# The last zero fill of a copy-bound kernel, dealt to fifteen of the sixteen DMA engines

**The chip, the cores and the metric.** One core of a Trainium2 chip. The metric is device microseconds (us) of one execution. Every timed execution here agreed within 0.3% with the others of its kernel and counts as undisturbed ("fast"), except the single runs of the last experiment, which are marked there. The times of one series come from one chip; the two timed series of experiments ran on two different chips.

## The reference

A single token goes through layernorm, attention over the last 4096 positions of a key and value cache, a residual, and a gated feed-forward network. The kernel must return the output row and eight gradients. Cut to what matters here:

```python
def _A_ref(x, k_cache, v_cache, wq, wo):
    Hq, Dh = 16, 256
    Hkv, Sk = k_cache.shape[1], k_cache.shape[2]      # 8, 32768
    W = min(4096, max(256, Sk // 4))                   # 4096
    k = jnp.repeat(k_cache[:, :, Sk - W:, :], rep, axis=1)
    v = jnp.repeat(v_cache[:, :, Sk - W:, :], rep, axis=1)
    ...
def reference(...):
    _out, _vjp = jax.vjp(_f, A_x, A_k_cache, A_v_cache, A_wq, A_wo, B_w_gate, B_w_up, B_w_down)
    _grads = _vjp(grad_out)
    return (_out0, *[jnp.asarray(_g) for _g in _grads])
```

The gradients of both caches have the shape of the caches, 1x8x32768x256 in bf16, and all but the last 4096 positions of each head are zero. Most of what the kernel writes is therefore zeros.

## The kernel before

A zero fill is a store of 128 rows of 8192 elements (`ZW`; 2 MB, 16,384 bytes in a row) from a tile of zeros in on-chip memory. GpSimd (`ZQ`) sends 103 of them, SyncE (`LD`) sends nearly all loads (ScalarE a few), all stores of results and the last few fills. Cuts are marked by `...`.

```python
ZW = 8192
HALF0, HALF1 = 42, 55
...
zeros = ar(0, ZW)                       # 128 partitions x ZW
...
late_jobs = [(out_2, G - 1, 5, 7, 2 * ZW), (out_3, G - 1, 0, 6, 2 * ZW), (out_3, G - 1, 6, 7, ZW)]
fills = []                              # the other 103 fills, [128, ZW] each
...
def send_fills(n0, n1, halves=False):
    for reg in fills[n0:n1]:
        if halves:
            ZQ.dma_start(out=reg.rearrange("p (k f) -> p k f", k=2),
                         in_=zeros[:, 0:ZW // 2].unsqueeze(1).to_broadcast([128, 2, ZW // 2]))
        else:
            ZQ.dma_start(out=reg, in_=zeros)

send_fills(0, HALF0)                    # 42 at the start
send_fills(HALF0, HALF1, True)          # 13 from half the tile
...
            if n == 1:                  # after the second block of the feed-forward part
                nc.vector.memset(ar(ZW // 2, ZW // 2), 0.0)
                send_fills(HALF1, len(fills))               # 48 more
...
for it, g in enumerate(order):          # backward, one key/value head at a time
    ...
    for o_ap, st_ in ((out_3, stV), (out_2, stK)):
        LD.dma_start(out=o_ap[0, g, Sk - W:, :].rearrange("(p t) d -> p t d", t=T), in_=st_)
    for job in plan[it]:
        job()
...
for o, g, n0, n1, f in late_jobs:       # the last stores of all
    reg = zero_rows(o, g, n0, n1, f)
    for i in range(reg.shape[0]):
        LD.dma_start(out=reg[i], in_=ar(2 * ZW - f, f))
```

Of the kernel before, what the change touches and what calls it, by code (L numbers as in the profile page):

```python
# [26 lines left out]
ZW = 8192  # L27
HALF0, HALF1 = 42, 55
# [5 lines left out]
def kernel(  # L34
# [4 lines left out]
    ZQ = nc.gpsimd  # L39
# [14 lines left out]
    def ar(off, n):  # L54
        return arena[:, off:off + n]
# [4 lines left out]
    zeros = ar(0, ZW)  # L60
# [54 lines left out]
    def zero_rows(o, g, n0, n1, f):  # L115
        reg = o[0, g, 0:Sk - W, :].rearrange("s d -> (s d)")[n0 * 128 * ZW:n1 * 128 * ZW]
        return reg.rearrange("(n p f) -> n p f", p=128, f=f)

    late_jobs = [(out_2, G - 1, 5, 7, 2 * ZW), (out_3, G - 1, 0, 6, 2 * ZW), (out_3, G - 1, 6, 7, ZW)]
    fills = []  # L120
# [7 lines left out]
# [3 lines that stand above are left out]
                ZQ.dma_start(out=reg.rearrange("p (k f) -> p k f", k=2), in_=zeros[:, 0:ZW // 2].unsqueeze(1).to_broadcast([128, 2, ZW // 2]))  # L131
            else:
                ZQ.dma_start(out=reg, in_=zeros)  # L133
# [212 lines left out]
    def block_views(n):  # L346
        f0, nb = BLOCKS[n]
        w = 128 * nb
        wgu = ar(wgu_off[n % 2], 8 * w).rearrange("p (c i f) -> p c i f", c=4, i=2)
        wd = ar(wd_off[n % 2], nb * D).rearrange("p (b n) -> p b n", n=D)  # L350
        return f0, nb, w, wgu, wd

    def load_block(n):
        f0, nb, w, wgu, wd = block_views(n)
        for eng, i, wt in ((LD, 0, B_w_gate), (nc.scalar, 1, B_w_up)):
            eng.dma_start(out=wgu[:, 0:3, i, :], in_=wt[0:384, :].rearrange("(c p) f -> p c f", c=3)[:, :, f0:f0 + w])
            eng.dma_start(out=wgu[0:DQ, 3, i, :], in_=wt[384:D, f0:f0 + w])
        LD.dma_start(out=wd, in_=B_w_down[f0:f0 + w, :].rearrange("(p b) n -> p b n", b=nb))
# [4 lines left out]
    with tc.tile_pool(name="ps_mid", bufs=3, space=bass.MemoryType.PSUM) as ps_mid, \  # L363
# [34 lines left out]
        for n in range(len(BLOCKS)):  # L398
            f0, nb, w, wgu, wd = block_views(n)
            b0 = f0 // 128  # L400
            cs = slice(b0, b0 + nb)
            for b in range(nb):
                nc.vector.tensor_tensor_reduce(out=dgb[:, 0:D], in0=wd[:, b, :], in1=dh2_bc[:], scale=1.0, scalar=0.0,
                                               op0=ALU.mult, op1=ALU.add, accum_out=d_hh[:, b0 + b:b0 + b + 1])
            gu_ps = ps_mid.tile([128, 2, 5], f32, tag="mid", name="gu_ps")
            for i in range(2):
                for b in range(nb):
                    for k in range(4):
                        kp = DQ if k == 3 else 128
                        nc.tensor.matmul(gu_ps[:, i, b:b + 1], lhsT=wgu[0:kp, k, i, b::nb], rhs=X2_b[0:kp, k:k + 1], start=(k == 0), stop=(k == 3))  # L410
            nc.vector.tensor_copy(out=gu_f[:, :, cs], in_=gu_ps[:, :, 0:nb])
            for i in range(2):
                nc.vector.tensor_tensor(out=dgu_f[:, i, cs], in0=d_hh[:, cs], in1=gu_f[:, 1 - i, cs], op=ALU.mult)
            nc.vector.tensor_tensor(out=hh_f[:, cs], in0=gu_f[:, 0, cs], in1=gu_f[:, 1, cs], op=ALU.mult)
            nc.vector.tensor_copy(out=hh_bf[:, cs], in_=hh_f[:, cs])
            for i in range(2):
                nc.vector.tensor_tensor(out=diag[:, 0:w].rearrange("p (m b) -> p m b", b=nb), in0=ident_f[:].unsqueeze(2).to_broadcast([128, 128, nb]),
                                        in1=dgu_f[:, i, cs].unsqueeze(1).to_broadcast([128, 128, nb]), op=ALU.mult)
                for m in range(2):
                    bc_ps = ps_mid.tile([128, 320], f32, tag="mid", name="bc_ps")  # L420
                    nc.tensor.matmul(bc_ps[:, 0:w // 2], lhsT=ones_bf[:], rhs=diag[:, m * w // 2:(m + 1) * w // 2], start=True, stop=True)
                    nc.scalar.copy(out=dgb[:, w * i + m * w // 2:w * i + (m + 1) * w // 2], in_=bc_ps[:, 0:w // 2])
            for b in range(nb):
                nc.tensor.matmul(ffn_ps[:], lhsT=hh_bf[:, b0 + b:b0 + b + 1], rhs=wd[:, b, :], start=(b0 + b == 0), stop=(b0 + b == NF - 1))
            for c in range(4):
                kp = DQ if c == 3 else 128
                wc = wgu[0:kp, c].rearrange("p i f -> p (i f)")
                nc.vector.tensor_tensor_reduce(out=wc, in0=wc, in1=dgb[0:kp, 0:2 * w], scale=1.0, scalar=0.0,
                                               op0=ALU.mult, op1=ALU.add, accum_out=dhn[0:kp, c, n:n + 1])
            if n + 2 < len(BLOCKS):  # L430
                load_block(n + 2)
            if n == 1:
                nc.vector.memset(ar(ZW // 2, ZW // 2), 0.0)
                send_fills(HALF1, len(fills))

        dcat2 = workm.tile([128, 8], f32)
        nc.vector.reduce_sum(out=dcat2[:, 0:4], in_=dhn[:], axis=AX)
# [57 lines left out]
    with tc.tile_pool(name="work2", bufs=2) as work2, tc.tile_pool(name="lnw", bufs=1) as lnw, \  # L495
# [109 lines left out]
        for it, g in enumerate(order):  # L605
# [50 lines left out]
            if it == 6:  # L656

                nc.vector.memset(ar(ZW, ZW), 0.0)

        for o, g, n0, n1, f in late_jobs:  # L660
            reg = zero_rows(o, g, n0, n1, f)
            for i in range(reg.shape[0]):
                LD.dma_start(out=reg[i], in_=ar(2 * ZW - f, f))
# [29 lines left out]
```

## Time and profile before

| | before |
|---|---|
| time, median (lowest to highest) | 798.80 us (798.65 to 799.12), 3 runs |
| span of the profiled execution | 797.2 us |
| moved by DMA | 334.76 MB, of them 280.59 MB written to memory |
| TensorE / VectorE / ScalarE busy | 60% / 55% / 25% |
| DMA engines busy | full until the last of forty slices |

No computing engine is busy for much more than half of the span, and the sixteen DMA engines are busy all the time. When the work is spread over sixteen servers that are all busy, an average rate tells nothing more: what matters is how ragged the end is, that is, how far apart the sixteen finish. The prediction below shows the lines for this, and how the ragged end is read: an engine alone is a share of 0.06 in the last stretches, and the last store's semaphore shows sixteen landings at the end. In the trace of before each of them comes 0.32 to 0.38 us after the end of one of the sixteen streams described next (the first streams end at 785.88 and 786.23 us, the first landings are at 786.22 and 786.55; the last 795.65 and 796.03), so they are read as one from each engine.

One piece of the reading is used throughout. The packets in the trace carry no engine number. But for 88% of the packets of 8,192 bytes or more between 400 and 780 us in the trace of before (8,376 of 9,478), some packet ends 3 to 4 ns after their start, and at 340 of 380 instants looked at there sixteen packets are in flight (at the others 17 or 18). This is read as one engine's next packet beginning 3 to 4 ns before the one before it ends, so packets can be strung into sixteen *streams*. A stream has no number either, but odd-sized packets can give one away. Where several packets end within a few ns, the order of the copies in each queue has to decide which stream goes on where, so a stream is an inference.

### The profile page before, as it was taken

The numbers are of one execution on the slowest core, as the hardware profiler recorded it, in microseconds if no ns is written. First come the engines' busy times: TensorE is split into PE (matmuls) and PEld (weight loads), VectorE is DVE, ScalarE is ACT, GpSimd is POOL, SyncE is SP. The second block draws the span as 40 slices with busy tenths as digits, with TensorE's granted clock in tenths as the row PEclk, the third lists the DMA queues.
The fourth block names the chain that finished last, engine by engine and source line by source line (L and its number), as shares of the span: only waits on it lengthen the run. The fifth ranks groups of instructions, "written<-read, shape, count | busy, mean of one in ns | idle before, by whom it ended". The sixth has DMA issues, their size and how long they took to land.

```text
span 797.2 us, 7318 instructions
## 1 busy us (share of the span) xinstructions
PE 478.9 (60%) x2926; PEld 222.6 (28%) x2926; DVE 437.1 (55%) x629; ACT 196.0 (25%) x309; POOL 61.8 (8%) x112
## 2 busy tenths in 40 slices
PE   0459999999999999251409478684450553722000
PEld 0334434344344333121208334331220211310000
DVE  2116584765846782263690679579653784964000
ACT  0142314134132201010102126353330442534000
POOL 4000000010101111100210001010000000000000
PEclk9989999999999999555558779766555556765555
DMA  9999999999999999999999999999999999999995
GB/s 349 431 430 430 428 431 430 430 428 430 430 423 427 427 419 413 423 421 424 432 428 423 424 431 431 428 425 427 424 424 422 424 424 424 423 427 418 433 434 247
DMA packets 29352, 334.76 MB, mean 420 GB/s; under 512 B 2819, under 2 KB 5894, under 8 KB 7814
## 3 DMA queue, kind: packets, MB, share of 16 engines
q0 software_dynamic: 16496, 216.01, 64.0%
q1 hardware_dynamic: 11382, 116.68, 34.8%
q10 hardware_dynamic: 1440, 1.61, 0.6%
q8 instruction: 23, 0.38, 0.2%
q14 instruction: 11, 0.09, 0.0%
HBM read 53.69 MB, written 280.59 MB: 419 GB/s over the span
## 4 chain that ended last, share of the span: by engine, by line
PE 37%; DMA 32%; DVE 16%; ACT 4%; issue 2%; another core or an unknown queue 0%; SPq 0%; DVEq 0%; ACTq 0%
DMA out_dram<-arena 19%; PE M_ps L317 12%; PE ok_ps L320 7%; PE rows_ps L256 6%; PE tr_ps L253 4%; DMA dh_bc<-in_grad_out_dram 4%; DMA arena<-in_A_k_cache_dram 4%; DMA arena<-in_B_w_down_dram 3%; ACT arena L270 2%; DVE arena L635 2%; DVE arena L459 2%; PE dqb_ps L502 2%; DMA arena<-in_B_w_gate_dram 2%; DVE arena L650 2%; PE d_ps L643 2%
## 5 line engine op out<-in xcount | busy, mean ns | idle before, releaser
L312 DVE TENSOR_TENSOR arena<-arena,p_f 128x2048 bf16<-128x2048 bf16 x64 | 145.4, 2286 | 61.6 <-PE M_ps L317 61.5
L317 PE MATMUL M_ps<-arena 128*128 128x512 bf16 x512 | 128.9, 380 | 0.2 <-ACT arena L323 0.2
L643 PE MATMUL d_ps<-arena,rT 32*128 32x512 bf16 x256 | 46.6, 529 | 111.0 <-DVE arena L651 63.9
L253 PE MATMUL tr_ps<-ident_bf,arena 128*128 128x128 bf16 x1024 | 92.5, 242 | 19.6 <-ACT arena L611 11.2
L256 PE MATMUL rows_ps<-arena,vpad 128*16 128x512 bf16 x256 | 90.6, 451 | 19.9 <-DVE arena L613 14.6
L133 POOL DMA_DIRECT2D out_dram<-arena x90 | 48.6, 542 | 538.5 <-DMA out_dram<-arena 491.3
L253 PEld LDWEIGHTS <-arena 128*128 128x128 bf16 x1024 | 69.0, 108 | 73.8 <-issue 64.4
L270 ACT COPY arena<-tr_ps 128x1024 bf16<-128x1024 bf16 x64 | 61.8, 1015 | 64.7 <-PE tr_ps L253 64.7
L647 ACT CAST arena<-d_ps 128x512 bf16<-128x512 f32 x64 | 37.7, 589 | 128.4 <-PE d_ps L643 128.3
L320 PE MATMUL ok_ps<-arena 128*16 128x512 bf16 x256 | 63.8, 381 | 0.9 <-DVE arena L297 0.9
L317 PEld LDWEIGHTS <-arena 128*128 128x128 bf16 x512 | 43.3, 99 | 59.0 <-issue 23.2
L611 ACT COPY arena<-tr_ps 128x1024 bf16<-128x1024 bf16 x32 | 32.6, 1019 | 94.6 <-PE tr_ps L253 36.4
L650 DVE CAST arena<-d_ps 128x512 bf16<-128x512 f32 x64 | 43.8, 684 | 16.9 <-PE d_ps L643 16.4
L651 DVE CAST arena<-d_ps 128x512 bf16<-128x512 f32 x64 | 43.5, 679 | 11.2 <-DMA out_dram<-arena 11.2
L643 PEld LDWEIGHTS <-rT 32*128 32x128 bf16 x256 | 11.2, 96 | 136.5 <-issue 90.0
L648 ACT CAST arena<-d_ps 128x512 bf16<-128x512 f32 x64 | 38.1, 595 | 11.9 <-DMA out_dram<-arena 11.9
L635 DVE TENSOR_TENSOR arena<-R_sb,tl_f 128x4096 bf16<-128x4096 bf16 x8 | 35.4, 4419 | 0.7 <-ACT R_sb L633 0.7
L256 PEld LDWEIGHTS <-vpad 128*16 128x16 bf16 x256 | 19.1, 92 | 58.4 <-issue 51.3
L320 PEld LDWEIGHTS <-arena 128*16 128x16 bf16 x256 | 19.1, 89 | 41.6 <-issue 20.5
L514 DVE CUSTOM_DVE_ANT_0 arena<-arena 128x4096 bf16<-128x4096 bf16 x3 | 13.1, 4423 | 23.9 <-ACT arena L507 23.9
L285 ACT ACTIVATE e_f<-cols_ps,nbias 128x32 f32<-128x32 f32 x16 | 4.5, 286 | 86.8 <-DVE nbias L281 86.8
L258 DVE COPY arena<-rows_ps 16x512 f32<-16x512 f32 x16 | 10.8, 676 | 26.6 <-PE rows_ps L256 26.6
(198 smaller groups left out, 387.9 us busy)
## 6 DMA issues: line engine op xcount, KB each, us to landing
out_dram<-arena POOLq DMA_DIRECT2D x103, 2048.0 KB, 51.7
out_dram<-arena SPq DMA_DIRECT2D x18, 2048.0 KB, 32.3
arena<-in_A_v_cache_dram SPq DMA_DIRECT2D x10, 2048.0 KB, 50.0
arena<-in_A_k_cache_dram SPq DMA_DIRECT2D x8, 2048.0 KB, 29.2
out_dram<-arena SPq DMA_DIRECT2D x4, 4096.0 KB, 43.8
arena<-in_A_wq_dram SPq DMA_DIRECT2D x2, 3072.0 KB, 20.6
arena<-in_A_wo_dram SPq DMA_DIRECT2D x2, 1792.0 KB, 14.5
out_dram<-arena SPq DMA_DIRECT2D x2, 1792.0 KB, 15.1
```

The lines of the kernel that those rows point to most:

```text
L133: ZQ.dma_start(out=reg, in_=zeros)
L253: nc.tensor.transpose(tr_ps[:, dh, i, :], X_sb[:, 4 * q + i, dh * 128:(dh + 1) * 128], ident_bf[:])
L256: nc.tensor.matmul(rows_ps[:], lhsT=pad[:, dh, 16 * q:16 * q + 16], rhs=XT[:, dh].rearrange("p t k -> p (t k)"), start=(q == 0 and dh == 0 ...
L270: sT_ps = dots(kv_at(K_off[g]), KT_slot, vpad[g % 2], rows1, ps_c, "cols", lambda q, XT, ps: nc.scalar.copy(out=XT, in_=ps))
L312: nc.vector.tensor_tensor(out=pK, in0=K_sb[:, 4 * c:4 * c + 4, :].unsqueeze(2).to_broadcast([128, 4, 2, Dh]), in1=p_f[:, c::8, :].unsqueez ...
L317: nc.tensor.matmul(M_ps[:, vh, :], lhsT=V_sb[:, t, vh * 128:(vh + 1) * 128], rhs=pK[:, i, :, :].rearrange("p h d -> p (h d)"), start=(t == ...
L320: nc.tensor.matmul(ok_ps[:].rearrange("p k d -> p (k d)"), lhsT=ppad[g % 2][:, 8 * (t % 4) + t // 4, :], rhs=both(g, t), start=(g == 0 and ...
L635: nc.vector.tensor_tensor(out=RB_, in0=R_sb[:].unsqueeze(1).to_broadcast([128, 8, 512]), in1=tl_f[:].unsqueeze(2).to_broadcast([128, 8, 51 ...
L643: nc.tensor.matmul(d_ps[:, qi].rearrange("p w d -> p (w d)"), lhsT=rT[32 * q:32 * (q + 1), :], rhs=RB_[32 * q:32 * (q + 1), l, :], start=T ...
L648: nc.scalar.copy(out=stK[:, t:t + 2, :], in_=d_ps[:, :, 1, :])
L650: nc.vector.tensor_copy(out=stV[:, t:t + 2, :], in_=d_ps[:, :, 0, :])
L651: nc.vector.tensor_copy(out=stK[:, t:t + 2, :], in_=d_ps[:, :, 1, :])
```

## The change

The intent: one of the sixteen engines is slower than the others and ends last. So the last of GpSimd's 103 fills is taken out of the loop, and sent at the very end in four parts that put rows on all engines but that one.

```diff
@@ -431,7 +431,7 @@
                 nc.vector.memset(ar(ZW // 2, ZW // 2), 0.0)
-                send_fills(HALF1, len(fills))
+                send_fills(HALF1, len(fills) - 1)
@@ -657,6 +657,14 @@
                 nc.vector.memset(ar(ZW, ZW), 0.0)
+        flat = fills[-1].rearrange("p f -> (p f)")
+        base = 0
+        for p0, k, m, w in ((0, 5, 2, 288), (20, 3, 8, ZW), (64, 8, 9, ZW - 40), (0, 4, 8, ZW)):
+            n = k * m * w
+            ZQ.dma_start(out=flat[base:base + n].rearrange("(k m f) -> k m f", k=k, m=m),
+                         in_=zeros[p0:p0 + 4 * k - 3:4, 0:w].unsqueeze(1).to_broadcast([k, m, w]))
+            base += n
+        assert base == 128 * ZW
         for o, g, n0, n1, f in late_jobs:
```

A tuple (p0, k, m, w) is one copy: m rows of w elements from each of k partitions p0, p0 + 4, p0 + 8 and so on. The engines are numbered here, as names: 0-4 (two tiny rows each), 5-7 (8 rows), 8-15 (9 rows, 40 elements shorter) and again 0-3 (8 rows). Engine 4 is the one that gets two rows of 576 bytes and no more. The stream with the two 896-byte stores is called engine 0.

## The prediction

> **What bounds the kernel now.** I read the page first, then busy time by stretch at the end, then GpSimd's timeline, and last the single landings and packets in the trace. The slices and queues of the page:
>
> ```profile
> PE   0459999999999999251409478684450553722000
> DMA  9999999999999999999999999999999999999995
> DMA packets 29352, 334.76 MB, mean 420 GB/s; under 512 B 2819, under 2 KB 5894, under 8 KB 7814
> q0 software_dynamic: 16496, 216.01, 64.0%
> q1 hardware_dynamic: 11382, 116.68, 34.8%
> ```
>
> The DMA engines are full in 39 of 40 slices, while TensorE has nothing to do in the last three. So the kernel is a copy: 334.76 MB (of which 216 MB zero fills from GpSimd on q0) over sixteen engines. What an engine does in which order hardly matters; the end is when the engine with most work left is done. The last stretches, in 1 us steps (us, five engines' busy time, clock, DMA share, GB/s):
>
> ```profile
> 782.00:784.00 2.00, 0.00 (x0) 0.00 (x0) 0.00 (x0) 0.00 (x0) 0.00 (x0) 0.50 0.97 418
> ...
> 788.00:789.00 1.00, 0.00 (x0) 0.00 (x0) 0.00 (x0) 0.00 (x0) 0.00 (x0) 0.50 0.65 279
> 789.00:790.00 1.00, 0.00 (x0) 0.00 (x0) 0.00 (x0) 0.00 (x0) 0.00 (x0) 0.50 0.27 115
> 790.00:791.00 1.00, 0.00 (x0) 0.00 (x0) 0.00 (x0) 0.00 (x0) 0.00 (x0) 0.50 0.12 49
> ...
> 793.00:794.00 1.00, 0.00 (x0) 0.00 (x0) 0.00 (x0) 0.00 (x0) 0.00 (x0) 0.50 0.11 49
> 794.00:795.00 1.00, 0.00 (x0) 0.00 (x0) 0.00 (x0) 0.00 (x0) 0.00 (x0) 0.50 0.04 16
> 795.00:796.00 1.00, 0.00 (x0) 0.00 (x0) 0.00 (x0) 0.00 (x0) 0.00 (x0) 0.50 0.04 16
> ```
>
> One engine is a share of 1/16 = 0.06. From 790 to 794 us two engines run (0.12), after that one, and the span ends at 797.2. The sixteen landings of the last store (its semaphore's events, in us from the span's start) say the same engine by engine: 786.2, 786.6, 787.2, 787.8, 787.8, 788.0, 789.2, 789.2, 789.5, 789.6, 789.8, 789.9, 790.4, 791.4, 794.4, 796.0. Their mean is 789.6, so perfect balance would be worth 796.0 - 789.6 = 6.4 us and no more. I call the last engine Z, the one of 794.4 Y, the one of 791.4 X.
>
> A packet of 16,384 bytes takes 0.611 us in the full stretches and also when Z runs alone, so an engine's own rate binds, and a row taken from Z is worth the same 0.611 us whenever it would have run.
>
> **Who Z is.** The packets carry no engine number, but on one engine the next packet starts 3 to 4 ns before the one before it ends, so they can be strung into sixteen streams, with the known order of every queue as a check. I followed them back from the end to 370 us. Z is not the stream with the two 896-byte stores of single rows (386 and 475 us)[...]. Z has no instruction fetch there, but its packets take 620 to 670 ns instead of 611 from 380 us on, when other engines' mostly do not: 5.9 us in all against 0.8 to 3.0 us on the others. Z is a steadily slow engine, not an unlucky one. The fetches[...] go round a set of eight streams, among them Y and X but neither Z nor engine 0.[...] The trace does not show that Z is the fifth (number 4); that the change aims so precisely at it is my main reason to believe it.
>
> [...]
>
> **The change, part by part.** The last of the 48 fills after the second block (128 rows of 16,384 bytes, 8 per engine) goes; four copies come, with k = 5, 3, 8, 4[...]. [...]engines 0 to 4 get 2 rows of 576 bytes each; 5 to 7 get 8 rows of 16,384; 8 to 15 get 9 rows of 16,304; 0 to 3 get 8 rows of 16,384. All 2 MB are covered.[...]
> - Engine 4: minus 8 x 0.611 = 4.89 us, plus 2 tiny packets, estimated at 0.04 us each from the 896-byte ones (41 ns). Net minus 4.8 us.
> - Engines 0 to 3 and 5 to 7: unchanged to 0.1 us.
> - Engines 8 to 15: 9 x 16,304 - 8 x 16,384 = 15,664 bytes more, 15,664 / 16,384 x 0.611 = 0.58 us[...].
>
> So if Z is engine 4 it lands at 796.0 - 4.8 = 791.2. The end then passes to Y: 794.4 if Y is in 0 to 7 (gain 1.6 us), 794.4 + 0.6 = 795.0 if it is in 8 to 15 (gain 1.0 us). X, at most at 792.0, is no issue. Two thirds of what is taken from Z is thus wasted.
>
> **GpSimd and the waits.** The last fills in GpSimd's timeline before:
>
> ```profile
> 664.67 0.53 POOL L133 DMA_DIRECT2D out_dram<-arena  x1 [9.41 <-DMA out_dram<-arena]
> 676.83 0.54 POOL L133 DMA_DIRECT2D out_dram<-arena  x1 [11.62 <-issue]
> ```
>
> It issues its last fill at 677 and is then idle. Four issues at 0.54 us are 2.2 us instead of 0.54, beside everything else. The built program shows new waits in front of the four: on VectorE's row copy (L258) and ScalarE's last transposed copy (L611) of the last group, which stand at about 701 us in the trace of before. So the fill comes some 25 us later. That costs nothing: in before the two preceding fills land at 718.6 and 724.7 us (median of their engines), SyncE's queue alone has work to 786, and the four need about 5 us of every engine somewhere before that. No other engine's instructions change place. SyncE's stores of the last groups may land up to 5 us sooner, which moves work but takes none away.
>
> **The rivals.**
> - *Aimed well, Y in 0 to 7*: gain 1.6 us, 797.2. *Aimed well, Y in 8 to 15*: gain 1.0 us, 797.8.[...]
> - *The wrong engine.*[...] Then Z keeps its 8 rows or gets 9: 798.8 to 799.5[...].
> - *Piled up.* If [...]each began at engine 0, engines 0 to 2 would get 8 + 9 + 8 rows instead of 8: 17 x 0.611 = 10.4 us more. Engine 0, ending at about 789.2, would land at about 799.6, and the time would be some 802.5. If Z were one of them, 809.
> - *A wait becomes the bound.* The four wait for late work; were SyncE's queue empty by then, they would be exposed. At 732 us, when TensorE is done, that queue is full to about 755, and its last stores are issued by 744, so I give this almost nothing.
>
> **Range and chances.** The timed runs spread by 0.5 us and sit 1.6 us above the span. I give the two aimed cases together 0.65 (797.2 and 797.8), the wrong engine 0.25 (798.8 to 799.5), piling up 0.07, anything else 0.03. The median of this is 797.8, and 797.0 to 799.5 holds a little over 8 in 10. Two per cent is 16 us, and the whole tail holds 6.4, so faster by 2% is out of reach. Slower by 2% needs the rows to collapse onto one or two engines.
>
> **What would show it.** Right: the last store's landings have a last value near 794.4 to 795.0 with the second near 792, one engine's share of 0.06 in the final 3 us in place of two engines' 0.12 at 790 to 794; the landings of eight engines 0.6 us later; on q0 the last 128 large packets on fifteen streams and none of them on Z. Wrong: a last landing still at 796.0 or later with Z having its 8 or 9 rows (wrong engine), or landings of three engines near 800 (piled up).[...]

That Z is engine 4, and that the four copies lie on the engines named, was not shown when the prediction was made. The rival *the wrong engine* is that the four copies spare another engine than Z. The stream with the two 896-byte stores, which the prediction goes on to call engine 0, lands at 789.2 us. The instruction fetches meant are the 23 packets of 16,384 bytes on q8, of the page's kind "instruction"; whose program they bring the page does not say.

The forecast's sum: Z lands at 796.0 - 8 x 0.611 + 2 x 0.04 = 791.2 us, so the end passes to Y, at 794.4 us or, with 0.58 us more, 795.0; that is 1.6 or 1.0 us off the 798.8 of before, 797.2 or 797.8 us.

## The result

| | before | after |
|---|---|---|
| time, median (lowest to highest), 4 runs each | 798.96 us (798.65 to 799.29) | 797.41 us (796.93 to 798.00) |
| span of the profiled execution | 797.2 us | 795.1 us |
| last landing / the one before it | 796.0 / 794.4 us | 794.0 / 793.3 us |
| mean of the sixteen landings | 789.6 us | 790.4 us |

The ratio is 0.9981, with a 95% interval of 0.9964 to 0.9998: a small gain of about 1.5 us, far within 2%. A ratio here is the mean time of one kernel's fast runs over that of the other's of the same rounds, so it isn't quite the ratio of the medians quoted.

The page of the kernel after, its DMA slices and queues:

```profile
DMA  9999999999999999999999999999999999999997
DMA packets 29688, 334.77 MB, mean 421 GB/s; under 512 B 3150, under 2 KB 6230, under 8 KB 8150
q0 software_dynamic: 16832, 216.01, 64.2%
q1 hardware_dynamic: 11382, 116.68, 35.0%
```

The same bytes are moved. The last slice is fuller, 7 tenths in place of 5: the engines now end closer together. There are 336 packets more on q0, and most are tiny: 320 more of 4 bytes (median 9 ns) and 11 of 8 bytes. In the kernel before, q0 has 1,648 packets of 4 bytes, one for each of 103 copies on 16 engines. After, it has 1,968, which are 272 beyond one for each of 106 copies on 16 engines, and 272 is 13 x 8 + 8 x 9 + 12 x 8: one for each row that the other engines got. For the first copy the 11 packets of 8 bytes fit, as many as there are other engines. So by these counts an engine without a share is not wholly idle, though at 9 ns a packet it is nearly so.

The last stretches of the kernel after, in the columns of the prediction (us, busy time of the five engines, clock, DMA share, GB/s):

```profile
788.00:789.00 1.00, 0.00 (x0) 0.00 (x0) 0.00 (x0) 0.00 (x0) 0.00 (x0) 0.50 0.77 328
789.00:790.00 1.00, 0.00 (x0) 0.00 (x0) 0.00 (x0) 0.00 (x0) 0.00 (x0) 0.50 0.54 229
790.00:791.00 1.00, 0.00 (x0) 0.00 (x0) 0.00 (x0) 0.00 (x0) 0.00 (x0) 0.50 0.31 131
791.00:792.00 1.00, 0.00 (x0) 0.00 (x0) 0.00 (x0) 0.00 (x0) 0.00 (x0) 0.50 0.31 131
792.00:793.00 1.00, 0.00 (x0) 0.00 (x0) 0.00 (x0) 0.00 (x0) 0.00 (x0) 0.50 0.08 33
793.00:794.00 1.00, 0.00 (x0) 0.00 (x0) 0.00 (x0) 0.00 (x0) 0.00 (x0) 0.50 0.04 16
```

Before, two engines ran alone from 791.1 us on. Now the share at 790 to 792 us is 0.31, about five engines' worth (5/16), and it falls to nothing within two more microseconds. The view counts whole packets: 0.08 is two packets of 0.61 us in one microsecond (2 x 0.61 / 16). The long tail of one engine is gone, and several others have taken its place.

GpSimd's timeline of the kernel after (start, us, engine, line, operation, number, and what ended the idle time before):

```profile
667.53 0.53 POOL L133 DMA_DIRECT2D out_dram<-arena  x1 [9.18 <-DMA out_dram<-arena]
701.35 1.94 POOL L664 DMA_DIRECT2D out_dram<-arena  x3 [33.30 <-DVE arena L651]
708.78 0.60 POOL L664 DMA_DIRECT2D out_dram<-arena  x1 [5.48 <-DMA out_dram<-arena]
```

The last ordinary fill goes out at 667.5 us and the four parts at 701 to 709 us, as foreseen. The releaser named in the brackets is inferred; the prediction read the waits, on VectorE's L258 and ScalarE's L611, from the built program.

**Which stream is which.** The last fill leaves marks, for on each group of engines its rows have another size. Five streams carry a packet of 1,152 bytes (two rows of 576 sent as one; 51 ns): they are engines 0 to 4. Eight carry nine packets of 16,304 bytes: 8 to 15. The one stream that has the 1,152-byte packet and no large row of this fill is engine 4. It is also the slow one: between 468 and 492 us, 36 of its 38 packets of 16,384 bytes took over 618 ns (Z before: 34 of 38), on the other fifteen streams together 5 of some 600. So Z of the prediction is engine 4. It is not slow all the time: its excess over 611 ns comes mostly between 380 and 560 us, at the same times in the traces of before, of the change and of its repeat, and from 740 us to the end none of its full packets is over 618 ns. It ends last because it fell behind earlier (by 5.9 us in all from 380 us on in the trace of before, against 0.8 to 3.0 us on the others). And the stream with the two 896-byte stores, the prediction's engine 0, is one of the four that got 8 rows beside their 1,152 bytes. In this profiled execution the four copies fell as the change assumes: the one engine spared is the slow one.

Engine 4's stream ended at 795.65 us before and at 791.46 us after, 4.2 us sooner. Who ends last now is engine 0 (793.65 us), then another of engines 0 to 3 (793.0), then one of 5 to 7 (792.5). The eight of engines 8 to 15, with their ninth row, end between 786.6 and 790.0 us.

### The profile page after: what moved, and what is told of

It reads as the page before. It is cut to its first block, busy times and chain, and to the rows that moved or that the text cites. A ratio compares the mean times of both kernels' runs of the same rounds, so it can differ in the third digit from the quotient of the medians.

```text
span 795.1 us, 7301 instructions
## 1 busy us (share of the span) xinstructions
PE 471.2 (59%) x2903; PEld 221.2 (28%) x2926; DVE 436.6 (55%) x629; ACT 196.0 (25%) x309; POOL 63.0 (8%) x115
## 4 chain that ended last, share of the span: by engine, by line
PE 35%; DMA 34%; DVE 15%; ACT 4%; issue 2%; another core or an unknown queue 0%; SPq 0%; DVEq 0%; ACTq 0%
DMA out_dram<-arena 21%; PE M_ps L317 12%; PE ok_ps L320 7%; PE rows_ps L256 5%; DMA dh_bc<-in_grad_out_dram 4%; DMA arena<-in_A_k_cache_dram 4%; PE tr_ps L253 4%; DMA arena<-in_B_w_down_dram 3%; ACT arena L270 2%; DVE arena L459 2%; PE dqb_ps L502 2%; DMA arena<-in_B_w_gate_dram 2%; DVE arena L635 2%; DVE arena L428 2%; DVE arena L650 1%
## 5 line engine op out<-in xcount | busy, mean ns | idle before, releaser
L317 PE MATMUL M_ps<-arena 128*128 128x512 bf16 x489 | 125.3, 381 | 1.9 <-issue 1.0
L253 PE MATMUL tr_ps<-ident_bf,arena 128*128 128x128 bf16 x1024 | 90.3, 239 | 19.7 <-ACT arena L611 11.4
L256 PE MATMUL rows_ps<-arena,vpad 128*16 128x512 bf16 x256 | 87.4, 436 | 21.0 <-DVE arena L613 15.2
L611 ACT COPY arena<-tr_ps 128x1024 bf16<-128x1024 bf16 x32 | 32.6, 1020 | 95.0 <-PE tr_ps L253 37.1
L258 DVE COPY arena<-rows_ps 16x512 f32<-16x512 f32 x16 | 10.8, 676 | 26.4 <-PE rows_ps L256 26.3
```

The costliest lines, as they stand in the source:

```text
L253: nc.tensor.transpose(tr_ps[:, dh, i, :], X_sb[:, 4 * q + i, dh * 128:(dh + 1) * 128], ident_bf[:])
L256: nc.tensor.matmul(rows_ps[:], lhsT=pad[:, dh, 16 * q:16 * q + 16], rhs=XT[:, dh].rearrange("p t k -> p (t k)"), start=(q == 0 and dh == 0 ...
L317: nc.tensor.matmul(M_ps[:, vh, :], lhsT=V_sb[:, t, vh * 128:(vh + 1) * 128], rhs=pK[:, i, :, :].rearrange("p h d -> p (h d)"), start=(t == ...
```

## The experiments

The first theory is the prediction's: the gain is the relief of engine 4, capped by the engines that come next. The rivals: the gain comes from the form or the late time of the fill, whoever gets the rows; or which partitions are read matters as well. All experiments but the last edit only the tuple of the four copies in the changed kernel, so the late sending and the waits stay. All results were correct. The kernel before, timed along with them, had a median of 799.03 us in the first series (the first four) and 798.94 us in the second (the next four), nine runs each.

### The changed kernel again

No edit.

> The changed kernel again, for a narrower interval. Both theories: 797.4 us, ratio 0.998. In the packet streams the slow stream (many packets of 620 to 670 ns between 380 and 560 us) gets one 1,152-byte packet and none of the last 128 large ones.[...]

Measured: 797.30 us (796.66 to 798.25), ratio 0.9979 [0.9966, 0.9991], span 794.9 us. The gain of 1.5 to 1.7 us is real. In this profile the last landings are 793.7 and 793.4 us, the mean of all sixteen 789.9 us. The stream that has only its 1,152 bytes of the last fill is again the slow one (36 of 38 over 618 ns), and ends at 790.8 us.

### Sixteen engines, all from one half of the partitions

```diff
-        ... in ((0, 5, 2, 288), (20, 3, 8, ZW), (64, 8, 9, ZW - 40), (0, 4, 8, ZW)):
+        ... in ((0, 16, 8, ZW),):
```

> The last fill as one copy in the same late place and the same strided form, with 16 source partitions, so 8 rows on each of the 16 engines. Theory 1 (the gain is the 8 rows that engine 4 no longer carries): the gain is gone, 799.0 us plus or minus 0.4, and the slow stream ends last again, 1 us or more behind the next. Rival (the gain comes from the fill being sent 25 us later, or in this form): 797.4.

Measured: 802.28 us (801.76 to 802.70), ratio 1.0041 [1.0028, 1.0053]. This misses what either theory expected: 3.3 us above before, with 8 rows meant for every engine just as before. The last landing is at 799.8 us and the mean of the sixteen at 795.1 us, 5.5 us later than before, so all engines lost time. The kernel with this edit, stretches while TensorE has its last work:

```profile
725.00:730.00 5.00, 1.84 (x12) 0.33 (x12) 2.92 (x5) 2.44 (x5) 0.00 (x0) 0.50 1.00 252
730.00:735.00 5.00, 0.61 (x4) 0.11 (x4) 2.24 (x4) 1.85 (x4) 0.00 (x0) 0.50 0.98 264
```

The engines are counted as full (1.00 and 0.98), yet they move 252 and 264 GB/s in place of the 415 and 418 that the kernel before moves in the same two stretches:

```profile
725.00:730.00 5.00, 1.34 (x12) 0.22 (x8) 3.44 (x6) 2.97 (x6) 0.00 (x0) 0.50 1.00 415
730.00:735.00 5.00, 0.61 (x4) 0.11 (x4) 1.71 (x3) 1.32 (x3) 0.00 (x0) 0.50 1.04 418
```

After 701 us, 99 of the large packets of GpSimd's queue took over 1,000 ns, typically 1,050 to 1,360 ns, where the usual time is 611 ns (in the kernel before, two of them did). What was overlooked is where the rows are read. Partitions 0, 4, ..., 60 all lie in the lower half, while in the change engines 0 to 7 read the lower half and 8 to 15 the upper, as the marks of the packets show. With the lower half alone the packets took about twice their usual time and the rate fell to 252 GB/s (with other traffic in the mix). That the source partitions are the cause is argued here; the two experiments on partitions below test it.

### Another engine skipped: number 12

```diff
-        ... in ((0, 5, 2, 288), (20, 3, 8, ZW), (64, 8, 9, ZW - 40), (0, 4, 8, ZW)):
+        ... in ((0, 13, 2, 144), (84, 3, 8, ZW), (0, 8, 9, ZW - 52), (64, 4, 8, ZW)):
```

> The same four-copy form, turned by eight: engine 12 gets no rows, engines 0 to 7 get 9 rows of 16,280 bytes. Theory 1: engine 4 has 0.6 to 0.7 us more than before and still ends last, so 799.5 us; the stream with the single tiny packet and no large rows is not the slow one. Rival (form or lateness gains): 797.4. Rival (the named engine is not 4[...]): anything else, and the streams tell.

Measured: 799.79 us (799.57 to 799.93), ratio 1.0009 [0.9996, 1.0023], which is 0.76 us above the median of before, a difference that the interval does not separate from none. The streams of this profile: the skipped one ends at 782.8 us, the first of all, and is not the slow one; the slow one is among engines 0 to 7 and got its ninth row. It ended at 796.48 us, 0.83 us later than before. The last stretches with this edit:

```profile
794.00:795.00 1.00, 0.00 (x0) 0.00 (x0) 0.00 (x0) 0.00 (x0) 0.00 (x0) 0.50 0.08 33
795.00:796.00 1.00, 0.00 (x0) 0.00 (x0) 0.00 (x0) 0.00 (x0) 0.00 (x0) 0.50 0.08 33
```

One engine is again alone (at most two packets in a microsecond). The form of the copies and their late time are those of the change; aiming them elsewhere takes the whole gain away. It must be the right engine that is spared.

### Half the rows back to engine 4

```diff
-        ... in ((0, 5, 2, 288), (20, 3, 8, ZW), (64, 8, 9, ZW - 40), (0, 4, 8, ZW)):
+        ... in ((0, 5, 4, ZW), (20, 3, 8, ZW), (64, 8, 17, ZW // 2), (0, 4, 4, ZW)):
```

Engine 4 now keeps four rows; 0 to 3 get 4 + 4, 5 to 7 get 8, and 8 to 15 get half a row more than before.

> Engine 4 keeps 4 of its 8 rows, engines 8 to 15 get 8.5 rows' worth. Theory 1 with the limit that the prediction names (the next engine then ends last): nearly the whole gain, 797.4 to 797.9. If engine 4 bound alone over its whole 4.9 us, half the gain: 798.2.

Measured: 797.00 us (796.85 to 797.40), ratio 0.9976 [0.9963, 0.9988]: the full gain, from half of the relief, and a little under the range expected. Engine 4's stream ends at 793.74 us, 1.9 us sooner than before, and is still the last, by 0.5 us. So beyond four rows nothing is gained for the time: the next engines hold it. This is the cap that the prediction argued with.

### The fill read from both halves of the partitions, 8 rows for each engine

```diff
-        ... in ((0, 5, 2, 288), (20, 3, 8, ZW), (64, 8, 9, ZW - 40), (0, 4, 8, ZW)):
+        ... in ((0, 8, 8, ZW), (64, 8, 8, ZW)):
```

> The control that the 16-partition copy failed to be: two copies of k = 8 in the late place[...], so 8 rows on each engine[...]. Theory 1 (only the rows taken off engine 4 gain): 799.0 plus or minus 0.5, the slow stream last. Rival (lateness or form gains): 797.4. Theory on the 16-partition copy[...]: no packet of the fill over 1,000 ns here but a handful.

The theory on the 16-partition copy is that its packets were slow because all its sources lay in one half.

Measured: 798.96 us (798.89 to 799.24), ratio 1.0000 [0.9988, 1.0013]. The kernel with this edit, GpSimd's timeline, then its middle and its last stretches:

```profile
705.06 1.17 POOL L664 DMA_DIRECT2D out_dram<-arena  x2 [40.84 <-DVE arena L651]
```

```profile
725.00:730.00 5.00, 1.84 (x12) 0.33 (x12) 2.88 (x6) 2.24 (x6) 0.00 (x0) 0.50 1.03 428
730.00:735.00 5.00, 0.61 (x4) 0.11 (x4) 2.51 (x4) 2.12 (x4) 0.00 (x0) 0.50 1.00 397
```

```profile
792.00:793.00 1.00, 0.00 (x0) 0.00 (x0) 0.00 (x0) 0.00 (x0) 0.00 (x0) 0.50 0.08 33
793.00:794.00 1.00, 0.00 (x0) 0.00 (x0) 0.00 (x0) 0.00 (x0) 0.00 (x0) 0.50 0.04 16
794.00:795.00 1.00, 0.00 (x0) 0.00 (x0) 0.00 (x0) 0.00 (x0) 0.00 (x0) 0.50 0.08 33
795.00:796.00 1.00, 0.00 (x0) 0.00 (x0) 0.00 (x0) 0.00 (x0) 0.00 (x0) 0.50 0.04 16
```

The fill goes out as late as in the change, reads the lower half for eight engines and the upper for the other eight, as the change does, and is meant to give every engine its 8 rows. The time is that of the kernel before, and the tail of one engine is back (last landing 796.3 us, the next 792.9 us). Lateness, waits and form are worth nothing that can be seen, to within 1 us either way by the interval. Beside the second experiment it shows what the source partitions do: the same sixteen times 8 rows, read from both halves, run at 428 and 397 GB/s, with two packets over 1,000 ns in place of 99.

### Rows as in the change, read from the other half

```diff
-        ... in ((0, 5, 2, 288), (20, 3, 8, ZW), (64, 8, 9, ZW - 40), (0, 4, 8, ZW)):
+        ... in ((64, 5, 2, 288), (84, 3, 8, ZW), (0, 8, 9, ZW - 40), (64, 4, 8, ZW)):
```

Every engine gets the same rows as in the change, but engines 0 to 7 read partitions 64 and up and engines 8 to 15 those from 0 on.

> The same rows on the same engines as in the change, but each source partition moved by 64[...]. [...]packets stay near 611 to 650 ns wherever the fill runs without SyncE's stores, and the time is 797.4 to 798.5. [...]packets of about 1,200 ns as in the 16-partition copy, and some 802.

The two outcomes: the first is for a swap that costs nothing in itself, the second for one that slows every row.

Measured: 805.69 us (805.20 to 806.05, four runs), ratio 1.0084 [1.0070, 1.0098], 6.7 us slower than before and some 8 us slower than the change (timed on another chip). It is above both outcomes expected. The kernel with this edit, two stretches:

```profile
725.00:730.00 5.00, 1.23 (x8) 0.22 (x8) 3.09 (x5) 2.49 (x5) 0.00 (x0) 0.50 1.02 268
735.00:740.00 5.00, 0.00 (x0) 0.00 (x0) 0.00 (x0) 0.00 (x0) 0.00 (x0) 0.50 0.97 277
```

The same picture as with one half alone: full shares and two thirds of the rate (the change moves 414 and 434 GB/s in these two stretches). Of the 72 rows of 16,304 bytes, 47 took over 1,000 ns; nine took 608 ns, about the usual 611. So the swap does not slow every row. Some of SyncE's stores at 739 to 744 us are as long, and come in pairs of equal times (1,199 and 1,200 ns; 1,251 and 1,252 ns). Why the swap slows the others is not shown. That the source partitions are what makes the difference is shown, since nothing else was changed: they are an essential part of the change, not a nicety.

### Moving rows off engines 0 to 7 as well

If engines 0 to 3 and 5 to 7 now end last and engines 8 to 15 have room, more should go from the former to the latter.

```diff
-        ... in ((0, 5, 2, 288), (20, 3, 8, ZW), (64, 8, 9, ZW - 40), (0, 4, 8, ZW)):
+        ... in ((0, 5, 2, 192), (20, 3, 6, ZW), (64, 8, 11, 7984), (0, 4, 6, ZW)):
```

> Engine 4 none, engines 0 to 3 and 5 to 7 six rows instead of eight, engines 8 to 15 eleven rows of 15,968 bytes. From the streams of the changed kernel (0 to 7 end at 789.5 to 793.6, 8 to 15 at 786.6 to 790.0): the first lose 1.2 us, the second gain 1.2, so the last is at about 792.4 and the time 796.2. If it does not gain, other engines than 0 to 7 end last by chance.

Measured: 795.55 us (795.25 to 796.46), ratio 0.9960 [0.9948, 0.9973].

```diff
-        ... in ((0, 5, 2, 288), (20, 3, 8, ZW), (64, 8, 9, ZW - 40), (0, 4, 8, ZW)):
+        ... in ((0, 5, 2, 384), (20, 3, 4, ZW), (64, 8, 13, 7840), (0, 4, 4, ZW)):
```

> Further the same way: four rows on engines 0 to 3 and 5 to 7, thirteen of 15,680 bytes on 8 to 15. The first end at 791.2 at the latest, the second 2.1 us later than in the changed kernel, 792.1 at the latest: 795.9 to 796.5, no better or little better than six rows, since 8 to 15 take over the end.

Measured: 795.58 us (794.38 to 795.93), ratio 0.9956 [0.9942, 0.9969]. Both beat both kernels (the changed kernel ran on another chip, but its fastest run, 796.66 us, is slower than the slowest of these, 796.46); the two can't be told apart. Both came out under what was expected of them. They take 3.4 us off the kernel before (798.94 - 795.55), twice what the change does. The last stretches with the second edit:

```profile
790.00:791.00 1.00, 0.00 (x0) 0.00 (x0) 0.00 (x0) 0.00 (x0) 0.00 (x0) 0.50 0.35 147
791.00:792.00 1.00, 0.00 (x0) 0.00 (x0) 0.00 (x0) 0.00 (x0) 0.00 (x0) 0.50 0.04 16
792.00:793.00 1.00, 0.00 (x0) 0.00 (x0) 0.00 (x0) 0.00 (x0) 0.00 (x0) 0.50 0.00 0
```

Over a third of the engines still work at 790 to 791 us and almost none a microsecond later. The streams end between 787.1 and 792.2 us, with engines 8 to 15 at 788.5 to 791.5 us. So the reason expected for no further gain, that 8 to 15 take over the end, did not hold: the last stream is still one of engines 5 to 7. The mean of the landings is 790.4 us and the last 792.6 us, so about 2.2 us is all that one more round of dealing could bring.

### Fills from SyncE's queue

This asks why engine 4 is slow. In the kernel *before*, the 48 later fills go through SyncE's queue in place of GpSimd's: 16 after the second block, and 4 at the start of each backward iteration.

```diff
-    def send_fills(n0, n1, halves=False):
+    def send_fills(n0, n1, halves=False, eng=None):
...
-                ZQ.dma_start(out=reg, in_=zeros)
+                (eng or ZQ).dma_start(out=reg, in_=zeros)
...
-                send_fills(HALF1, len(fills))
+                send_fills(HALF1, HALF1 + 16, eng=LD)
...
+            send_fills(HALF1 + 16 + 4 * it, HALF1 + 20 + 4 * it, eng=LD)
```

> A look, not a race: the 48 fills after the second block are issued by SyncE, so that GpSimd sends nothing from about 365 us on. If engine 4 is slow because of GpSimd's copies, then after GpSimd's last fill has landed no one stream has packets of 620 to 670 ns that the others lack; in the kernel before, 34 of the slow stream's 38 packets between 468 and 492 us were over 618 ns and hardly any of the others' were. If it is slow whatever issues the copies, one stream still has most of its 16,384-byte packets over 618 ns while VectorE is busy. The time may be anything from 800 to 950 us[...].

Measured: 819.11 us against 799.17 us for before on the same chip, one run each, whose state is unknown; the time isn't used. Its page, queues:

```profile
q1 hardware_dynamic: 18294, 217.34, 63.0%
q0 software_dynamic: 9584, 115.35, 33.3%
```

Half of GpSimd's bytes have moved to SyncE's queue. In two stretches with not one packet of GpSimd in flight, 410 to 440 us and 440 to 465 us, one stream has 34 of 48 and 33 of 38 of its 16,384-byte packets over 618 ns (means 626 and 636 ns), and all the others together two and four, single packets of 879 to 1,018 ns, where the usual time is 611 ns. In the kernel before, with GpSimd's fills in flight, it was 34 of 38 (mean 640 ns) at 468 to 492 us. So the slowness does not need copies of GpSimd in flight. That the slow stream of this run is number 4 is likely, but nothing in it shows the number. What makes the engine slow stays open.

## Why the prediction was right or wrong, point by point

The time was predicted as 797.8 us, within 797.0 to 799.5. It came out as 797.41 and, in the repeat, 797.30 us.

- **What bounds the kernel.** Right. Sparing one engine moves the end (the change), sparing another does not (number 12), and spreading better moves it further (the two last edits of the tuple).
- **Who Z is.** Right that Z is engine 4, which was given two thirds (the author's estimate). The stream of engine 4 is the slow one in the profile after, by its packet marks. "Steadily slow" is too much: its packets stand out only from 380 to 560 us. It does have one instruction fetch, by my stringing (8 KB at 560.6 us, 420 ns), which is too little to matter. Nor did only two engines run from 790 us: X ended at 791.1 us. The guess that Y and X are in 8 to 15 was taken from the eight streams that the instruction fetches of 16,384 bytes go round, and was not shown. By the marks of the change and of the second moving edit, these eight are two of engines 5 to 7 and six of 8 to 15. They take the fetches in turn, and by its turn Y is one of 5 to 7, and so is X. So the end of 797.2 us, not 797.8 us, was the one that the prediction's own sum gives for the case at hand.
- **Engine 4 loses 4.8 us.** Right: its stream ends 4.2 us sooner, and 4.8 us in the repeat (4.9 by rows; between single executions). The half edit scales: four rows are 2.4 us by the same working, and 1.9 us were measured.
- **Engines 8 to 15 gain 0.58 us.** The size fits: in the experiment that skipped number 12 the slow stream took this extra row, with 0.83 us on its stream and 0.76 us on the time, in single executions and within the noise. Nothing beyond the bytes was seen clearly: rows of 16,304 bytes took 627.0 ns in one profile and 620.6 ns in the other, GpSimd's full rows beside them, between 722.4 and 732.1 us, 621.2 and 619.1 ns.
- **The end passes to Y.** This step failed. The prediction took the order of the field in one profile as fixed, with Y at 794.4 to 795.0 us and the second at about 792. Measured were 794.0 and 793.3 us, with engine 0, which ended at 789.2 us before, last. Three of engines 0 to 3, matched between the traces by their instruction fetches and the 896-byte stores, were already about 3 us behind their place of before at 640 us, ahead of anything that the change does, while Y, with the same rows as before, ended 1.6 us sooner. Single engines vary so from one execution to the next: in the two profiles of the changed kernel engine 0 ended at 793.65 and at 790.90 us. What holds the end after engine 4 is the latest of several engines, which landed at 793.7 and 794.0 us in these profiles, whoever it was. That is near to where Y stood. So the mechanism (a cap by the next engines) was right and its term was put on the wrong engine; that the time came out within 0.5 us is in part luck.
- **Two thirds of the relief wasted.** Right: half of it gives all the gain.
- **The waits cost nothing.** Right: with 8 rows on each engine, the late fill costs 0.0 us, to within 1 us.
- **The source partitions.** The prediction had one sentence on them and gave them no weight at all. What follows when other partitions are read should have been a rival: read from one half, the fill costs 3.3 us more than before; from the halves swapped, 6.7 us. Both are larger than the whole gain.
- **The rivals.** *The wrong engine* is refuted for the profiled executions by the marks, and an engine spared that changed from execution to execution would have spread the runs by some 2.5 us (an estimate from 797.30 us with engine 4 spared and 799.79 with number 12); the spread of the change is 1.1 and 1.6 us in its two series against 0.5 to 0.9 us before, so that unprofiled executions always spare engine 4 isn't shown. *Piled up* is refuted: the 1,152-byte packets lie on five streams, and the large rows on the groups meant for them. *A wait as the bound* is refuted as said.

## What to carry to other kernels

When a kernel is bound by full DMA engines, read the sixteen landings of its last transfer: their last value minus their mean (6.4 us here, of which dealing by hand brought 3.4) is all that better dealing can bring. A copy whose source is the same for all rows could here be cut into parts of k partitions (5, 3, 8 and 4) to give chosen engines more or less. But which partitions each part is read from counts for more than the balance gives: all from the lower half cost 3.3 us and the halves swapped 6.7 us, against a gain of 1.6. Don't aim only at the engine that is last in one profile: the slow one was slow in every trace read for it, the rest change places by some microseconds, so the goal is a level field with room where it varies.
